# Pooled attention into a gated feed-forward layer: one matmul for each odd score, exponentials in groups of 16, even and odd tokens in turn

## The chip, the cores and the metric

One core of a Trainium2 chip runs the whole program. In this kernel TensorE does the matmuls, into buffers in PSUM memory; ScalarE does the exponentials and relu; VectorE and GpSimd do sums and products of elements. The metric is the device time of one execution in microseconds; the span of a profile, from the first to the last instruction of the core, is about 1.8 us shorter. Runs come in states; only fast runs are compared here, and of read_fours, a single run of unknown state, only the trace is read.

## The reference, cut to what matters

```python
# q, k, v: (8 batches, 8 heads, 576 tokens, 64)
k_p = k.reshape(B, H, Sp, 8, D).mean(axis=3)        # 72 pooled positions
v_p = v.reshape(B, H, Sp, 8, D).mean(axis=3)
scores = np.matmul(q, k_p.transpose(0, 1, 3, 2)) / np.sqrt(D)
attn = softmax(scores)                               # over 72 positions
x = np.matmul(attn, v_p)                             # -> (4608 tokens, 512)
out = (np.maximum(x @ w_gate, 0) * (x @ w_val)) @ w_out   # 512 -> 1536 -> 512
```

A caution about correctness: on these inputs the output has a standard deviation of 1.26e-5, and the spread between tokens of one batch is only 6.1e-8, half a per cent of that (computed from the reference). The comparison with the reference passes even when tokens of a batch are exchanged. A pass says little about the order of rows, which has to be checked by following the indices.

## The kernel before

A q tile holds two tokens side by side in the 128 rows: rows 0 to 63 are an even token, rows 64 to 127 the odd one after it. The pooled keys are kept twice, with zeros in the upper or the lower half, so that one matmul scores the even tokens (`j == 0`) and another the odd ones (`j == 1`). A batch has 18 column groups of 16 columns; 16 of these make the full blocks, 2 are the leftover. The value matmuls take blocks of 128 tokens as weights, and each block must lie in one piece. The leftover block takes 32 even and 32 odd tokens, and so the odd half stores its leftover first, next to the even one. That is why an odd score was two matmuls: its columns come in another order than they lie in q.

```python
def scores(b, h, j):
    n = RI * QP                                       # 2 * 16 = 32
    ...
    parts = ((n, 0, NF * IQ), (0, NF * IQ, RI)) if j else ((0, 0, NI),)
    ps = ps_at.tile([P, 512], F32, name="at_ps", tag="at_ps")
    for c0, i0, cnt in parts:                         # odd: 256 columns, then 32
        nc.tensor.matmul(
            out=ps[:SP, c0:c0 + cnt * QP], lhsT=kpTs[b % 2][j][:, h, :],
            rhs=queries(b, h, i0, cnt), start=True, stop=True)
    e = exp_tiles[b, h][:SP, j * HS:(j + 1) * HS]
    ...                                               # batch 7: two permuted views
    for out_ap, in_ap in views:
        nc.scalar.activation(out=out_ap, in_=in_ap, func=AF.Exp, scale=EXP_SCALE)

def weights(b, h, t):                                 # the weights of value block t
    ...
    n_blk, j = divmod(t, 2)                           # a block is all even or all odd
    c0 = NF * P if t == n_pc - 1 else (HS + RI * QP if j else 0) + n_blk * P
    return exp_tiles[b, h][:SP, c0:c0 + n]
```

Batch 0 goes another way and is not touched. Scores of a batch are put in groups of two (batch 1) or mostly three (later batches) between the matmuls of the feed-forward part.

The softmax here doesn't subtract the row's maximum and nothing guards it: scores larger than these inputs give would overflow.

## Time and profile before

| | before |
|---|---|
| median of the first 3 runs | 328.61 us (328.54 to 330.12) |
| TensorE busy | 318.7 us, 97% |
| ScalarE busy | 151.2 us, 46% |
| scores, batches 1 to 7, between starts of matmuls | 15.39 us |
| exponentials, batches 1 to 6 | 96 of 288 elements, 402 ns each |

The prediction below shows the lines of the page, the groups and the timeline. One view more: what TensorE waited for in the kernel before (who waited for whom: us in total, times, longest).

```profile
PE acc_ps L523 <- DVE sum L514: 0.3, 1, 0.3
PE at_ps L311 <- ACT expT L325: 0.2, 1, 0.2
```

The first line is a place where VectorE is the later one; the second is all that TensorE ever waited for an exponential.

### The profile page before, as it was taken

How to read it: one execution, taken by the hardware profiler on the slowest of the kernel's cores; microseconds unless marked ns; L12 is line 12 of the kernel's file. 1: busy time of each engine (PE TensorE's matmuls, PEld its weight loads, DVE VectorE, ACT ScalarE, POOL GpSimd, SP SyncE). 2: the span in 40 equal slices, each digit the busy share in tenths (PEclk: the TensorE clock that was granted, in tenths of full speed). 3: DMA queues.
4: the chain of work that ended last, by engine and by line, in shares of the span. 5: the costliest groups of instructions: out<-in, count | busy, mean ns of one | idle time of the engine just before them, and what ended most of it. 6: DMA issues, size and time to landing. Idle time of an engine off the chain costs nothing.

```text
span 327.4 us, 7013 instructions
## 1 busy us (share of the span) xinstructions
PE 318.7 (97%) x2670; PEld 226.9 (69%) x2670; DVE 226.2 (69%) x482; ACT 151.2 (46%) x353; POOL 206.9 (63%) x258
## 2 busy tenths in 40 slices
PE   8899999999999999999999999999999999999995
PEld 3577885455566656665898867655667888888674
DVE  7465737677684864696387745784779989879762
ACT  1454482364466226612672257225825565565330
POOL 8556607999999942965199309999901577667300
PEclk9999999999999999999999999999999999999999
DMA  7999998996958538999794472223012130130035
GB/s 110 186 203 202 200 211 151 200 173 118 187 101 159 100 91 86 78 154 160 159 169 76 87 104 60 33 47 124 3 24 50 34 96 2 22 111 2 10 112 137
DMA packets 51010, 35.46 MB, mean 108 GB/s; under 512 B 30432, under 2 KB 45024, under 8 KB 50976
## 3 DMA queue, kind: packets, MB, share of 16 engines
q0 software_dynamic: 18304, 18.88, 36.5%
q1 hardware_dynamic: 32528, 16.00, 26.2%
q8 instruction: 21, 0.34, 0.4%
q10 hardware_dynamic: 144, 0.13, 0.1%
q14 instruction: 13, 0.11, 0.1%
HBM read 37.75 MB, written 9.44 MB: 144 GB/s over the span
## 4 chain that ended last, share of the span: by engine, by line
PE 89%; DVE 6%; DMA 2%; issue 1%; POOL 1%; ACT 0%; DVEq 0%; POOLq 0%
PE mm_ps L430 42%; PE acc_ps L523 19%; PE mm_ps L742 9%; PE at_ps L311 4%; PE mm_ps L468 3%; PE at_ps L389 3%; PE mm_ps L602 2%; DMA q<-in_q_dram 2%; PE at_ps L742 2%; DVE px L395 1%; DVE sum L514 1%; DVE h L439 1%; PE mm_ps L412 1%; PE mm_ps L366 1%; DVE px L758 1%
## 5 line engine op out<-in xcount | busy, mean ns | idle before, releaser
L439 DVE TENSOR_TENSOR h<-mm_ps,relu 128x512 f16<-128x512 f32 (+1 forms) x96 | 59.8, 624 | 69.5 <-PE mm_ps L430 59.2
L436 ACT ACTIVATE relu<-mm_ps 128x512 f16<-128x512 f32 (+1 forms) x96 | 52.2, 544 | 100.1 <-PE mm_ps L430 94.6
L430 PE MATMUL mm_ps<-x_T,wv_sb 128*128 128x512 f16 (+1 forms) x432 | 88.4, 332 | 0.4 <-DVE kpT0u L264 0.4
L430 PE MATMUL mm_ps<-x_T,wg_sb 128*128 128x512 f16 (+1 forms) x432 | 88.5, 331 | 0.0
L430 PEld LDWEIGHTS <-wv_sb 128*128 128x128 f16 x432 | 42.1, 98 | 31.2 <-DVE kpT0u L264 0.8
L430 PEld LDWEIGHTS <-wg_sb 128*128 128x128 f16 x432 | 38.9, 97 | 19.7 <-issue 0.3
L325 ACT ACTIVATE expT<-at_ps 72x288 f16<-72x288 f32 (+2 forms) x128 | 38.8, 374 | 14.3 <-PE at_ps L311 14.2
L523 PEld LDWEIGHTS <-sum 128*128 128x128 f16 x336 | 32.0, 98 | 6.3 <-DVE sum L514 0.9
L395 DVE TENSOR_TENSOR px<-at_ps,prd 128x256 f16<-128x256 f32 (+1 forms) x80 | 33.8, 423 | 2.7
L181 POOL TENSOR_TENSOR tree_b<-tree_a 72x256 f32<-72x256 f32 (+1 forms) x42 | 33.5, 797 | 3.3
L764 POOL TENSOR_TENSOR h<-px 128x256 f16<-128x256 f16 x36 | 25.4, 718 | 13.8 <-ACT px L761 12.8
L175 POOL TENSOR_TENSOR tree_a<-k_in 96x512 f32<-96x512 f16 x18 | 21.5, 1196 | 15.2 <-DMA k_in<-in_k_dram 15.2
L523 PE MATMUL acc_ps<-wo_sums,sum 128*128 128x256 f16 x252 | 30.9, 272 | 0.0
L175 POOL TENSOR_TENSOR tree_a<-v_in 72x512 f32<-72x512 f16 x24 | 28.7, 1197 | 0.1
L523 PEld LDWEIGHTS <-h 128*128 128x128 f16 x252 | 23.7, 98 | 2.9
L763 POOL TENSOR_SCALAR px<-px 128x256 f16<-128x256 f16 x12 | 13.0, 1080 | 18.1 <-PE mm_ps L742 15.3
L844 POOL COPY gate<-h 128x1 f16<-128x1 f16 x4 | 1.5, 380 | 33.9 <-DVE h L439 33.9
L523 PE MATMUL acc_ps<-wo_sb,h 128*128 128x256 f16 x168 | 20.6, 272 | 0.0
L514 DVE TENSOR_TENSOR sum<-h 128x768 f16<-128x768 f16 x28 | 19.0, 679 | 0.0
L531 DVE TENSOR_TENSOR rows<-acc_ps,mid 128x512 f32<-128x512 f32 x21 | 14.4, 686 | 4.7 <-PE acc_ps L523 4.6
L389 PEld LDWEIGHTS <-expT 72*128 72x128 f16 (+1 forms) x280 | 12.9, 100 | 5.9 <-DVE prd L394 0.8
L394 DVE RECIPROCAL prd<-at_ps 128x4 f32<-128x4 f32 (+1 forms) x80 | 13.7, 171 | 3.7 <-PE at_ps L389 3.6
(144 smaller groups left out, 527.9 us busy)
## 6 DMA issues: line engine op xcount, KB each, us to landing
out_dram<-rows SPq DMA_DIRECT2D x24, 256.0 KB
k_in<-in_k_dram POOLq DMA_DIRECT2D x7, 576.0 KB, 7.0
q<-in_q_dram POOLq DMA_DIRECT2D x7, 576.0 KB, 10.0
v_in<-in_v_dram POOLq DMA_DIRECT2D x6, 576.0 KB, 12.7
wg_sb<-in_moe_w_gate_dram POOLq DMA_DIRECT2D x6, 256.0 KB, 11.0
wv_sb<-in_moe_w_val_dram POOLq DMA_DIRECT2D x6, 256.0 KB, 10.8
wo_sb<-in_moe_w_out_dram POOLq DMA_DIRECT2D x3, 512.0 KB, 10.7
v_in<-in_v_dram POOLq DMA_DIRECT2D x2, 512.0 KB, 11.9
```

What stands on the lines that cost most here:

```text
L175: eng.tensor_tensor(out=cell["a"][:n], in0=src[:, :, :4 * D], in1=src[:, :, 4 * D:], op=ALU.add)
L181: eng.tensor_tensor(out=cell["c"][:n], in0=a[:n, :, :2 * D], in1=a[:n, :, 2 * D:], op=ALU.add)
L325: nc.scalar.activation(out=out_ap, in_=in_ap, func=AF.Exp, scale=EXP_SCALE)
L389: nc.tensor.matmul(out=ps[:n, c0:c0 + D + 1], lhsT=weights(b, h, t), rhs=stats[b % 2][:SP, g, s0:s0 + D + 1], start=True, stop=True,)
L395: nc.vector.tensor_tensor(out=x[:n, half * NG // 2:(half + 1) * NG // 2, :, :], in0=pv.rearrange("p g (x c) -> p g x c", x=2)[:, :, :, :D] ...
L430: nc.tensor.matmul(out=t[:, lo:hi], lhsT=w[:, ci, fsl], rhs=x_T[:, ci, x0:x0 + hi - lo], start=(ci == 0), stop=(ci == n_co - 1),)
L436: nc.scalar.activation(out=relu[:, :n], in_=ps[0][:, :n], func=AF.Relu)
L439: nc.vector.tensor_tensor(out=h_tiles[c][:, fo, t0:t0 + n], in0=ps[1][:, :n], in1=relu[:, :n], op=ALU.mult)
L514: nc.vector.tensor_tensor(out=S[k][:, i], in0=x[:, i], in1=y[:, i], op=op)
L523: nc.tensor.matmul(out=ps[:, tb, :], lhsT=lhs[:, i, tb * P:(tb + 1) * P], rhs=rhs[:, i, :], start=(first and tb == 0 and i == 0), stop=(tb ...
L742: nc.tensor.matmul(out=ps[key][:, m], lhsT=w_of(m)[:, i], rhs=xs[:, i], start=(first and m == 0 and i == 0), stop=(m == 1 and i == N_CO - ...
L764: nc.gpsimd.tensor_tensor(out=hc[:, fo_out, cols], in0=gv[:, 0], in1=gv[:, 1], op=ALU.mult)
```

## The change

Its intent is that an odd score is one matmul, as an even one is. The exponentials of a head are stored as 18 groups of 16 even, 16 odd tokens, so any block of 128 columns holds both kinds and the leftover is simply the end. The price: each activation writes 16 elements, leaves out 16, and so on (in batch 7: every second element), and the rows of the output go to other places.

```diff
-        parts = ((n, 0, NF * IQ), (0, NF * IQ, RI)) if j else ((0, 0, NI),)
-        ps = ps_at.tile([P, 512], F32, name="at_ps", tag="at_ps")
-        for c0, i0, cnt in parts:
-            nc.tensor.matmul(... queries(b, h, i0, cnt) ...)
-        e = exp_tiles[b, h][:SP, j * HS:(j + 1) * HS]
+        ps = ps_at.tile([P, 512], F32, name="at_ps", tag="at_ps")[:SP, :HS]
+        nc.tensor.matmul(
+            out=ps, lhsT=kpTs[b % 2][j][:, h, :], rhs=queries(b, h), start=True, stop=True)
+        e = exp_tiles[b, h][:SP]
+        def blocks(cols):
+            return e[:, cols].rearrange("s (i j p) -> s i j p", j=2, p=QP)[:, :, j]
+        ps = ps.rearrange("s (i p) -> s i p", p=QP)
+        views = [(blocks(slice(0, 2 * HS)), ps)]
         if b == LAST:
+            views = [(blocks(rest), ps[:, i:]),
+                     (e[:, full].rearrange("s (t p i j) -> s t p i j", ...)[:, :, :, :, j],
+                      ps[:, :i].rearrange("s (t i) p -> s t p i", i=TP // 2))]
 ...
-        c0 = NF * P if t == n_pc - 1 else (HS + RI * QP if j else 0) + n_blk * P
-        return exp_tiles[b, h][:SP, c0:c0 + n]
+        return exp_tiles[b, h][:SP, t * P:t * P + n]
 ... (stores: rows of a block are now neighbours in memory; the leftovers of a
      batch are one store of 64 rows where they were two of 32)
```

More of the change, by code (lines that the diff above doesn't have):

```diff
@@ L108 @@
     out_rows_of = out.rearrange("(b p i j) d -> b j i p d", j=2, i=NI, p=QP)
-    out_cols_of = out.rearrange("(b p i j) d -> b j p i d", j=2, i=NI, p=QP)
+    out_runs_of = out.rearrange("(b p r) d -> b r p d", r=QT, p=QP)
+    out_cols_of = out.rearrange("(b p r) d -> b p r d", r=QT, p=QP)
+    TP = P // QP
     def full_at(b):
@@ L301, in scores @@
     def scores(b, h, j):
-        n = RI * QP
         if j == 0:
@@ L307, in scores @@
                 "s j p -> s (j p)")
-        parts = ((n, 0, NF * IQ), (0, NF * IQ, RI)) if j else ((0, 0, NI),)
-        ps = ps_at.tile([P, 512], F32, name="at_ps", tag="at_ps")
-        for c0, i0, cnt in parts:
-            nc.tensor.matmul(
-                out=ps[:SP, c0:c0 + cnt * QP], lhsT=kpTs[b % 2][j][:, h, :],
-                rhs=queries(b, h, i0, cnt), start=True, stop=True,
-            )
-        e = exp_tiles[b, h][:SP, j * HS:(j + 1) * HS]
-        ps = ps[:SP, :HS]
-        views = [(e, ps)]
-        if b == LAST:
-            rest = slice(0, n) if j else slice(HS - n, HS)
-            full = slice(n, HS) if j else slice(0, HS - n)
-            views = [(e[:, rest], ps[:, rest]),
-                     (e[:, full].rearrange("s (k p i) -> s k p i", k=NF, i=IQ),
-                      ps[:, full].rearrange("s (k i p) -> s k p i", k=NF, i=IQ))]
+        ps = ps_at.tile([P, 512], F32, name="at_ps", tag="at_ps")[:SP, :HS]
+        nc.tensor.matmul(
+            out=ps, lhsT=kpTs[b % 2][j][:, h, :], rhs=queries(b, h), start=True, stop=True)
+        e = exp_tiles[b, h][:SP]
+        full, rest = slice(0, 2 * NF * P), slice(2 * NF * P, None)
+        def blocks(cols):
+            return e[:, cols].rearrange("s (i j p) -> s i j p", j=2, p=QP)[:, :, j]
+        ps = ps.rearrange("s (i p) -> s i p", p=QP)
+        views = [(blocks(slice(0, 2 * HS)), ps)]
+        if b == LAST:
+            i = 2 * NF * P // (2 * QP)
+            views = [(blocks(rest), ps[:, i:]),
+                     (e[:, full].rearrange("s (t p i j) -> s t p i j", p=QP, j=2, i=TP // 2)[
+                         :, :, :, :, j],
+                      ps[:, :i].rearrange("s (t i) p -> s t p i", i=TP // 2))]
         for out_ap, in_ap in views:
@@ L331, in weights @@
             return pieces[t][:SP, h, :n]
-        n_blk, j = divmod(t, 2)
-        c0 = NF * P if t == n_pc - 1 else (HS + RI * QP if j else 0) + n_blk * P
-        return exp_tiles[b, h][:SP, c0:c0 + n]
+        return exp_tiles[b, h][:SP, t * P:t * P + n]
     def pool_v_array(b, half):
@@ L445, in store @@
         if rest % P == (REST if b % 2 else 0) and (b % 2 or rest < FULL):
-            n, j = divmod((r0 - full_at(b)) // P, 2)
-            nc.sync.dma_start(out=out_rows_of[b, j, n * IQ:(n + 1) * IQ], in_=o)
+            t = (r0 - full_at(b)) // P
+            n, j = divmod(t, 2)
+            to = out_runs_of[b, t * TP:(t + 1) * TP] if b else \
+                out_rows_of[b, j, n * IQ:(n + 1) * IQ]
+            nc.sync.dma_start(out=to, in_=o)
         else:
             half = RI * QP
-            for x in range(4):
-                nc.sync.dma_start(
-                    out=out_rows_of[b + x // 2, x % 2, NF * IQ:], in_=o[x * half:(x + 1) * half])
+            for x in range(2):
+                if b + x:
+                    nc.sync.dma_start(
+                        out=out_runs_of[b + x, 2 * NF * TP:], in_=o[x * REST:(x + 1) * REST])
+                    continue
+                for j in range(2):
+                    nc.sync.dma_start(
+                        out=out_rows_of[0, j, NF * IQ:], in_=o[j * half:(j + 1) * half])
     def store_cols(o, t, eng, cols):
-        n, j = divmod(t, 2)
-        eng.dma_start(out=out_cols_of[LAST, j, :, n * IQ:(n + 1) * IQ, cols], in_=o)
+        eng.dma_start(out=out_cols_of[LAST, :, t * TP:(t + 1) * TP, cols], in_=o)
     def out_rows(c, ts, eng=None):
```

## The prediction

> **What bounds the kernel now.** I read first the busy shares and the chain that ended last on the page, because they say which engine's time is the kernel's time.
>
> ```profile
> PE 318.7 (97%) x2670; PEld 226.9 (69%) x2670; DVE 226.2 (69%) x482; ACT 151.2 (46%) x353; POOL 206.9 (63%) x258
> ...
> PE 89%; DVE 6%; DMA 2%; issue 1%; POOL 1%; ACT 0%; DVEq 0%; POOLq 0%
> ```
>
> TensorE is busy for 97% of the span and carries 89% of the chain; ScalarE is busy for 46% and carries none of it. A busy TensorE is not proof of a bound, since ends of matmuls are modelled, so the second view is busy time by stretch, over the stretches in which batches 2 to 7 are scored (columns: stretch, length, then busy time and count of PE, PEld, DVE, ACT, POOL, granted clock, DMA share, GB/s).
>
> ```profile
> 80.00:120.00 40.00, 39.95 (x311) 24.38 (x308) 29.72 (x66) 17.21 (x37) 35.92 (x46) 1.00 0.70 129
> 120.00:160.00 40.00, 40.00 (x303) 25.76 (x302) 25.19 (x49) 18.12 (x38) 19.63 (x25) 1.00 1.03 131
> 200.00:240.00 40.00, 39.73 (x297) 24.71 (x296) 26.41 (x50) 19.60 (x60) 35.73 (x33) 1.00 0.18 42
> ```
>
> TensorE has no gap there, at full clock, and the list of waits gives TensorE only 0.2 us of waiting on ScalarE in the whole run. So what the change saves on TensorE should come off the end nearly in full, and what it costs ScalarE should be hidden. The third view says how big the thing removed is: the groups of the scores, each shape apart.
>
> ```profile
> L311 PE MATMUL at_ps<-qT,kpT1l 128*72 128x288 f16 x32 | 9.1, 290 | 0.0
> L311 PE MATMUL at_ps<-qT,kpT1u 128*72 128x256 f16 x32 | 8.7, 273 | 0.2 <-ACT expT L325 0.2
> ...
> L311 PE MATMUL at_ps<-qT,kpT1u 128*72 128x32 f16 x32 | 5.7, 179 | 0.0
> ...
> L311 PE MATMUL at_ps<-qT,kpT0u 128*72 128x32 f16 x24 | 4.3, 179 | 0.0
> ```
>
> The trap is here. The two groups of 32 columns, 32 + 24 = 56 matmuls, show 5.7 + 4.3 = 10.0 us of busy time. That is not what they cost: 179 ns is the latency of one, and the next matmul starts long before it ends. What a matmul costs a full TensorE is the distance to the next start, which the timeline shows (start, length, engine, line, operation; "x2" is the pair of 256 and 32 columns of one odd score).
>
> ```profile
> 127.39 0.29 PE L311 MATMUL at_ps<-qT,kpT0l 128*72 128x288 f16 x1
> 127.51 0.29 PE L311 MATMUL at_ps<-qT,kpT0u 128*72 128x256 f16 x2
> 127.65 0.29 PE L311 MATMUL at_ps<-qT,kpT0l 128*72 128x288 f16 x1
> 127.78 1.03 PE L430 MATMUL mm_ps<-x_T,wg_sb 128*128 128x512 f16 x4
> 128.64 1.03 PE L430 MATMUL mm_ps<-x_T,wv_sb 128*128 128x512 f16 x4
> 129.51 0.29 PE L311 MATMUL at_ps<-qT,kpT0u 128*72 128x256 f16 x2
> ```
>
> An even score (one matmul of 288 columns) holds TensorE for 127.51 - 127.39 = 0.12 us, an odd one (two matmuls) for 127.65 - 127.51 = 0.14 us. The even score after it takes 0.13. The removed matmul is worth some hundredths of a microsecond each, not 0.18.
>
> **What the Trainium skill says.** "TensorE: Matmul & The Clock Gate", section "Wait — 56ns, not 53.3ns?", has warm matmuls start N/2.4 GHz + about 2.5 ns apart, and never closer than about 25 ns however small N is. This trace agrees: the starts, read to the nanosecond, are 123 ns apart after 288 columns (288/2.4 + 2.5 = 122.5), 109 after 256 (109.2), and 28 after 32 columns, where the formula alone would give 15.8: the floor. "ScalarE: Activation LUTs", section "What ACT_TABLE_LOAD costs", has an activation with immediate operands take 186 ns + 0.833 ns per element, with about 93 ns overlapped back to back. For 288 that is 426, and 333 in a row; the trace has 402 and, between starts in a row, 290, a little less. "SBUF — State Buffer", section "Door 1: The DMA port swizzle", says that SBUF works in lines of 16 bytes and that at least two hits per line keep full bandwidth. No instruction of this trace writes groups as short as the new ones, so the trace neither confirms nor denies it.
>
> **The change, part by part.**
>
> 1. Removed on TensorE: in each of 7 batches x 8 heads = 56 odd scores, the second matmul and its weight load. The built instruction order of the two kernels agrees: 112 rows fewer on TensorE. Before, an odd score costs 109 + 28 = 137 ns; after, as one matmul of 288 columns, 123. That is 14 ns x 56 = 0.78 us.
>
> 2. A shadow of it: the score that follows a 32-column matmul takes 129 ns rather than 123[...]. Thirty even scores follow an odd one directly: 6 ns x 30 = 0.18 us. Parts 1 and 2 make 0.96 us of a TensorE that has no gaps.
>
> 3. Moved on ScalarE: for batches 1 to 6 each exponential writes 18 groups of 16 f16 (32 bytes, with 32 bytes between them) rather than 288 in a row; for batch 7 it writes every second f16. Same count, same elements. The groups of the exponentials now:
>
> ```profile
> L325 ACT ACTIVATE expT<-at_ps 72x288 f16<-72x288 f32 x96 | 32.5, 402 | 13.0 <-PE at_ps L311 13.0
> ...
> L325 ACT ACTIVATE expT<-at_ps 72x256 f16<-72x256 f32 x16 | 5.8, 384 | 0.0
> ```
>
> The 256-element form of batch 7 already reads PSUM with a stride of 64 bytes, and its successor starts 264 ns later, which is 290 - 32 x 0.833 = 263: a strided read costs nothing. For the write, 16 f16 fill two whole 16-byte lines, and every second f16 still leaves four per line, so by the page above both stay at full rate. I choose no change, and at most 10%. The tightest place for ScalarE is batch 1, where two scores follow every half-size gate and value pair:
>
> ```profile
> 43.47 0.70 ACT L325 ACTIVATE expT<-at_ps 72x288 f16<-72x288 f32 x2 [0.16 <-PE at_ps L311]
> 44.07 0.38 ACT L436 ACTIVATE relu<-mm_ps 128x256 f16<-128x256 f32 x1
> 44.60 0.70 ACT L325 ACTIVATE expT<-at_ps 72x288 f16<-72x288 f32 x2 [0.16 <-PE at_ps L311]
> ```
>
> The period is 44.60 - 43.47 = 1.13 us, with 0.16 us idle. Two exponentials take 2 x 0.29 = 0.58 us of it, so they would have to slow by 0.16/0.58 = 28% before ScalarE set the pace even there. Elsewhere three of them and one 0.6 us relu share 2.1 us or more.
>
> 4. Moved in waits: a block of values now holds even and odd tokens, so the first block of batches 2, 4 and 6 needs the last odd exponential too; in the built order just three weight loads gain a wait on ScalarE. In these batches a whole gate and value unit (1.7 us) lies between the last score and the first value block, against an exponential of 0.4 us and a relu of 0.6. It costs 0.
>
> 5. Output: 7 fewer stores of the small kind (four of 32 rows become two of 64), the same 2 KB rows, now adjacent in memory. The queue that issues them mostly waits for data, and only the last store is on the path: same size, 1 KB pieces as before. It costs 0.
>
> Sum: 0.96 us off. I let a tenth of it be absorbed in the few places where TensorE waits on VectorE anyway (0.35 us at 65 us is one), so 0.9: 328.61 - 0.9 = 327.7 us, 0.3%.
>
> **Rivals.** (a) The busy-time reading: 56 x 179 ns = 10 us off, 318.6. Against it stands the 0.14 against 0.12 us of the timeline; I give it nearly nothing. (b) The scattered write is slow. If each element cost twice as much, an exponential would grow by 0.24 us; in batch 1 a pair and its relu would need about 0.58 + 0.48 + 0.38 = 1.4 us against 1.13, 0.3 us x 8 rounds = 2.4 us later, and batch 7, with 0.36 us idle of each 2.13 us period, would lose about 1 more: 331, 1% slower. Only the missing precedent for such a write speaks for it. (c) Nothing comes through: each saving of 40 ns per trio is swallowed by the next wait, 328.6. The gapless stretches speak against it. (d) Stores to adjacent rows land sooner or later than before: they are hidden, at most 0.3 us at the tail either way.
>
> **Range and chances.** The three runs of before span 328.54 to 330.12, so noise of some tenths is as large as the effect. 327.0 to 328.8 holds the sum in full, nothing, and a small loss. Neither side reaches 2% (6.6 us) by any step worked out here: faster 0.01, same 0.97, slower 0.02.
>
> **What would show it.** Right: the 32-column groups are gone, all 112 scores have one shape, a trio falls from 0.39-0.40 to 0.37 us between starts, the exponentials still take about 0.40 us, and TensorE's waits on ScalarE stay near 0.2 us. Wrong: exponentials of 0.45 us and more, starts in a row over 0.32 us, a wait of TensorE on ScalarE of more than 1 us in batch 1 or 7, or a saving of TensorE over 2 us.

## The result, and the profile after

| | before | after |
|---|---|---|
| median, fast runs of these rounds | 328.88 us (4 runs) | 327.90 us (4 runs) |
| ratio, 95% interval | | 0.9968 (0.9948 to 0.9988) |
| the same in a second set of rounds | 329.10 us (11 runs) | 328.29 us (5 runs), 0.9972 (0.9958 to 0.9986) |

A ratio here is formed from the fast runs of the same rounds; it is not quite the ratio of the medians. The changed kernel is 0.3% faster: clear of noise, and "same" by a limit of 2%.

The page of the changed kernel, busy shares and chain:

```profile
PE 316.8 (97%) x2614; PEld 224.7 (69%) x2614; DVE 226.6 (69%) x482; ACT 151.9 (47%) x353; POOL 206.2 (63%) x258
...
PE 88%; DVE 6%; DMA 2%; issue 1%; ACT 1%; POOL 1%; DVEq 0%; ACTq 0%; POOLq 0%
```

There are 2670 - 2614 = 56 matmuls fewer, and the bound is where it was. TensorE's busy time fell by 1.9 us, the span of this execution by 0.9: as the prediction warned, busy time of matmuls is no measure of what they cost. Of the 1.9 us, 1.1 lie in the 28 warm-up matmuls at the start (10.1 us before, 9.0 after), which the change does not touch. The groups of the odd scores in the changed kernel, by form:

```profile
L310 PE MATMUL at_ps<-qT,kpT1u 128*72 128x288 f16 x32 | 8.9, 287 | 0.2 <-ACT expT L327 0.2
...
L310 PE MATMUL at_ps<-qT,kpT0u 128*72 128x288 f16 x24 | 6.6, 286 | 0.0
```

The rows of 256 and of 32 columns are gone. The timeline of the first group of batch 4 answers to that of the prediction (start, length, what):

```profile
127.17 0.29 PE L310 MATMUL at_ps<-qT,kpT0l 128*72 128x288 f16 x1
127.29 0.29 PE L310 MATMUL at_ps<-qT,kpT0u 128*72 128x288 f16 x1
127.42 0.29 PE L310 MATMUL at_ps<-qT,kpT0l 128*72 128x288 f16 x1
127.54 1.03 PE L430 MATMUL mm_ps<-x_T,wg_sb 128*128 128x512 f16 x4
```

Three scores hold TensorE for 127.54 - 127.17 = 0.37 us, where it was 127.78 - 127.39 = 0.39. Taking each score's distance to the next matmul from the starts in the trace, all 112 scores took 15.39 us before and 14.40 after: 0.99 us less, in which the waits inside the stages are counted too. The stretches from a batch's first score to the first matmul after its last one sum to 68.62 us before and 67.67 after, 0.95 us less.

On ScalarE, the exponentials of batches 1 to 6 and of batch 7:

```profile
L327 ACT ACTIVATE expT<-at_ps 72x288 f16<-72x288 f32 x96 | 32.6, 403 | 12.6 <-PE at_ps L310 12.0
L327 ACT ACTIVATE expT<-at_ps 72x256 f16<-72x256 f32 x16 | 6.5, 461 | 0.0
```

Groups of 16 cost nothing: 403 ns against 402, and 290 ns between starts in a row as before. Batch 7's did slow down, from 384 to 461 ns, and from 264 to 304 ns between starts. Nobody waits for it: TensorE's waits of the changed kernel have the same line for exponentials as before.

```profile
PE acc_ps L530 <- DVE sum L521: 0.7, 2, 0.3
...
PE at_ps L310 <- ACT expT L327: 0.2, 1, 0.2
```

The first line is the small part of the gain that did not arrive. TensorE now waits 0.7 us for VectorE's sums rather than 0.3, because it comes there earlier while VectorE's work is what it was. Of the six stretches from the end of one batch's scores to the start of the next, the two with these waits grew from 22.51 to 22.66 us and from 22.58 to 22.63: 0.20 us given back. after_again shows 22.66 and 22.62. The sum of all six is no such witness: it was 129.99 us before, 130.14 after, and 129.78 in after_again, because the first stretch alone was 18.55, 18.49 and 18.15 us.

### The profile page after: what moved, and what is told of

Same layout as the page of the kernel before. It is cut to its first block, busy times and chain, and to the rows that moved or that the text cites. A ratio compares the mean times of both kernels' runs of the same rounds, so it can differ in the third digit from the quotient of the medians.

```text
span 326.5 us, 6890 instructions
## 1 busy us (share of the span) xinstructions
PE 316.8 (97%) x2614; PEld 224.7 (69%) x2614; DVE 226.6 (69%) x482; ACT 151.9 (47%) x353; POOL 206.2 (63%) x258
## 4 chain that ended last, share of the span: by engine, by line
PE 88%; DVE 6%; DMA 2%; issue 1%; ACT 1%; POOL 1%; DVEq 0%; ACTq 0%; POOLq 0%
PE mm_ps L430 42%; PE acc_ps L530 19%; PE mm_ps L749 9%; PE at_ps L310 4%; PE mm_ps L475 3%; PE at_ps L389 3%; PE mm_ps L609 2%; PE at_ps L749 2%; DMA q<-in_q_dram 2%; DVE px L395 1%; DVE sum L521 1%; DVE h L439 1%; PE mm_ps L412 1%; DVE px L765 1%; PE mm_ps L284 1%
## 5 line engine op out<-in xcount | busy, mean ns | idle before, releaser
L430 PEld LDWEIGHTS <-wg_sb 128*128 128x128 f16 x432 | 40.0, 98 | 20.7 <-issue 0.4
L327 ACT ACTIVATE expT<-at_ps 72x288 f16<-72x288 f32 (+2 forms) x128 | 39.7, 384 | 13.4 <-PE at_ps L310 12.7
## 6 DMA issues: line engine op xcount, KB each, us to landing
wo_sb<-in_moe_w_out_dram POOLq DMA_DIRECT2D x3, 512.0 KB, 10.1
```

What stands on the lines that cost most here:

```text
L430: nc.tensor.matmul(out=t[:, lo:hi], lhsT=w[:, ci, fsl], rhs=x_T[:, ci, x0:x0 + hi - lo], start=(ci == 0), stop=(ci == n_co - 1),)
```

## The experiments

Theory: the saving is the TensorE time of 56 small matmuls and nothing else, and the new way of writing is hidden behind TensorE. Rivals: the saving comes from the stores to adjacent rows or from the layout; ScalarE is near its limit and only just hides the new writes. All ratios are against the kernel before of the same rounds.

**after_again: the changed kernel once more**, without an edit.

> The changed kernel once more, to narrow the interval. If the saving is the 0.96 us of TensorE counted in the prediction and nothing else, the ratio to the kernel before is 0.997 (0.9 to 1.0 us less). If the first measurement was noise, the ratio lies within 0.001 of 1.

Ratio 0.9972 (0.9958 to 0.9986), five runs of 327.88 to 328.47 us against eleven of 328.51 to 329.92. The saving is not noise.

**split_odd: undo only the merging.**

```diff
+        cut = NF * IQ
+        for i0, cnt in ((0, cut), (cut, RI)) if j else ((0, NI),):
+            nc.tensor.matmul(
+                out=ps[:, i0 * QP:(i0 + cnt) * QP], lhsT=kpTs[b % 2][j][:, h, :],
+                rhs=queries(b, h, i0, cnt), start=True, stop=True)
```

> The changed kernel with one thing undone: each odd score is two matmuls again (256 and 32 columns), the layout of the exponentials, the blocks and the stores stay new. Theory (the matmul count is the whole saving): the scores take 15.4 us between starts again instead of 14.4, and the time goes back to that of the kernel before, ratio 0.999 to 1.001. Rival (the saving comes from the stores to adjacent rows, or from the new layout): the ratio stays at 0.997.

Ratio 0.9998 (0.998 to 1.0015); the scores take 15.40 us between starts, the score stages 68.62 us, both as in the kernel before. The first group of batch 4 holds TensorE for 128.25 - 127.86 = 0.39 us again:

```profile
127.86 0.29 PE L312 MATMUL at_ps<-qT,kpT0l 128*72 128x288 f16 x1
127.99 0.29 PE L312 MATMUL at_ps<-qT,kpT0u 128*72 128x256 f16 x2
128.12 0.29 PE L312 MATMUL at_ps<-qT,kpT0l 128*72 128x288 f16 x1
128.25 1.03 PE L433 MATMUL mm_ps<-x_T,wg_sb 128*128 128x512 f16 x4
```

With new layout and new stores but two matmuls, the saving is gone. The rivals of stores and layout fall.

**merge_only: do only the merging**, in the kernel before.

```diff
-        parts = ((n, 0, NF * IQ), (0, NF * IQ, RI)) if j else ((0, 0, NI),)
+        parts = ((0, 0, NI),)
```

> The kernel before with one thing done: an odd score is one matmul of 288 columns, layout and stores stay old. The odd tokens land in wrong blocks, so the result is wrong on purpose. Theory: the whole saving, ratio 0.997, scores 14.4 us between starts. Rival (stores or layout): ratio 1.000.

Ratio 0.9983 (0.9966 to 1.0; one of six runs was slow and is left out). By its time alone this run decides nothing, since the interval holds both 0.997 and 1. The trace is plainer: the scores take 14.40 us between starts and the stages 67.67 us, the same as in the changed kernel. In the profiled execution half a microsecond was lost elsewhere; the view of waits has a line that neither of the two kernels has.

```profile
PE mm_ps L430 <- DMA x_T<-px: 0.4, 1, 0.4
```

This is a transposing transfer that landed late once. Whether it did so in the other runs the times don't say.

**split_all: a double dose**, every score of the changed kernel in two matmuls.

```diff
+        for i0, cnt in ((0, cut), (cut, RI)):
```

> The changed kernel with every score split into 256 and 32 columns, even ones too: a double dose of what the change removed. Theory: 112 small matmuls at 14 ns net each and a shadow of about 6 ns on the matmul after each is 2.2 us more than the changed kernel, 1.2 us more than the kernel before: ratio 1.003 to 1.004. Rival (the split costs nothing, the layout does): ratio 0.997. Busy-time rival (179 ns for each): ratio above 1.03.

Ratio 1.0003 (0.9989 to 1.0017): the expected size was missed. The timeline shows that the dose itself was taken, three scores now from 127.81 to 128.23, 0.42 us:

```profile
127.81 0.29 PE L312 MATMUL at_ps<-qT,kpT0l 128*72 128x256 f16 x2
127.94 0.29 PE L312 MATMUL at_ps<-qT,kpT0u 128*72 128x256 f16 x2
128.09 0.29 PE L312 MATMUL at_ps<-qT,kpT0l 128*72 128x256 f16 x2
128.23 1.02 PE L433 MATMUL mm_ps<-x_T,wg_sb 128*128 128x512 f16 x4
```

The score stages sum to 69.58 us, 1.91 more than in the changed kernel (2.2 was expected, with 6 ns of delay behind each of the 112 small matmuls; the trace has such a delay mainly where another score follows directly, 66 times, where 256 columns take 115 or 116 ns rather than 109). Of that the time shows some 1.0 us. The waits for VectorE's sums, 0.7 us in the changed kernel, are not in this kernel's list of waits at all, and the stretches in which they lie shrank from 22.66 and 22.63 us to 22.25 and 22.14, by 0.41 and 0.49. So VectorE is a second limit close behind TensorE in two of the six stretches between the scores: what one makes TensorE slower, up to about 0.4 us a stretch, comes back there, and what one makes it faster is in part lost there.

**step_two and read_fours: which side of batch 7's activation became slow.** It reads PSUM in fours with a stride of 64 bytes (before: in eights), and it writes every second f16 (before: in a row). step_two gives the write alone to batches 1 to 6; read_fours leaves batch 7 the read alone. Both leave tokens in wrong places.

```diff
 # step_two
-        views = [(blocks(slice(0, 2 * HS)), ps)]
+        views = [(e.rearrange("s (i p j) -> s i p j", j=2, p=QP)[:, :, :, j], ps)]
 # read_fours
-                     (e[:, full].rearrange("s (t p i j) -> s t p i j", ...)[:, :, :, :, j],
+                     (e[:, j * NF * P:(j + 1) * NF * P].rearrange(
+                         "s (t p i) -> s t p i", p=QP, i=TP // 2),
```

> The changed kernel, but in batches 1 to 6 each exponential reads PSUM in a row and writes every second f16, as batch 7 does; the stores are left, so the order of the rows is wrong on purpose. It asks which side of batch 7's activation made its successor start 303 ns later instead of 264. If the write at every second f16 is it (39 ns for 256 elements), the 288-element ones go from 290 to about 334 ns between starts and from 403 to about 490 ns each. If the read in fours from PSUM is it, they stay at 290 and 403. In both cases ScalarE has slack and the ratio stays at 0.997.

> The changed kernel, but in batch 7 the exponential of 256 elements writes them in a row while it still reads PSUM in fours with a stride of 64 bytes; wrong values on purpose. If the write at every second f16 costs the 39 ns, the time between starts goes back to 264 and its length to about 383; if the read in fours costs it, they stay at 303 and 460.

The groups of the exponentials, step_two first (its batches 1 to 6), then read_fours (its batch 7):

```profile
L327 ACT ACTIVATE expT<-at_ps 72x288 f16<-72x288 f32 x96 | 38.0, 483 | 11.1 <-PE at_ps L310 10.2
```

```profile
L327 ACT ACTIVATE expT<-at_ps 72x256 f16<-72x256 f32 x16 | 5.8, 385 | 0.0
```

With the write at every second f16, 288 elements take 483 ns rather than 403, and 322 to 334 between starts in a row, most often 326, rather than 290 or 291. Without it, batch 7 is back at 385 and 264. It is the write. The time of step_two is 0.9976 (0.9959 to 0.9992), as good as the changed kernel's: even 96 slowed exponentials are hidden. Its score stage of batch 1, the tightest for ScalarE, is 8.46 us against 8.38, so some 36 ns more per exponential are just felt there.

**exp_twice_b1: a dose for ScalarE where it is tightest.**

```diff
-        for out_ap, in_ap in views:
+        for out_ap, in_ap in views * (2 if b == 1 else 1):
```

> The changed kernel, with each exponential of batch 1 done twice to the same place: a dose of 2 x 290 ns in each of 8 periods of 1.13 us in which ScalarE is idle for 0.16. The prediction's claim is that ScalarE sets the pace once a pair grows by more than 0.16 us. Then each period grows by 0.58 - 0.16 = 0.42 us, 2.5 to 3.4 us in all: ratio 1.005 to 1.008. If ScalarE is not near its limit there, the ratio stays at 0.997.

Ratio 1.0316 (1.0278 to 1.0355): the sign was right, the size far off. The local part came as expected: the score stage of batch 1 grew from 8.38 to 11.65 us, by 3.27. The rest of it is in the waits of TensorE.

```profile
PE at_ps L310 <- DMA qT<-q: 6.0, 1, 6.0
PE at_ps L310 <- ACT expT L327: 2.7, 6, 0.7
```

The second line is the delay that was put in. The first is new: batch 2's queries, transposed by a transfer, are not there. The chain of waits shows the transfer and what follows it (start, length, what):

```profile
58.72 17.33 DMA qT<-q
76.05 0.04 issue
76.09 0.88 PE at_ps L310 x3
76.97 2.56 PE mm_ps L475 x6
```

In the changed kernel this transfer is issued at 54.6 us and nobody waits for it at 66.0. Here it is issued at 58.7 and lands only 17.3 us later, in a stretch in which the DMA engines are full (shares of 0.93 and 1.22 in the view by stretch). But they are hardly less full in the changed kernel (0.88 to 1.01 from 54.6 to 76 us). What differs is the order: there the transfer is issued 3.1 us before the next loads of k, q and v from GpSimd's queue (57.7, 58.2 and 58.8 us), here in their midst (58.3, 58.8 and 59.4). In its first 4.1 us there, the transfer's queue (q1) has 70% of the DMA engines' time and GpSimd's (q0) 6%; in its first 7.3 us here, 25% and 68%. And while TensorE waits, its granted clock falls: it is 0.50 from 76 to 80 us, where six matmuls of 512 columns take 2.56 us instead of 1.30. A delay of 3.3 us became 11 us. No run isolates what made the transfer slower; that the loads were no longer behind it is the likely cause, and this is argued from the two traces, not shown.

**half_array: an attempt to beat both**, without the zeros: even scores on the lower 64 rows of the array, odd ones on the upper 64.

```diff
+        ds = slice(D, P) if j else slice(0, D)
         nc.tensor.matmul(
-            out=ps, lhsT=kpTs[b % 2][j][:, h, :], rhs=queries(b, h), start=True, stop=True)
+            out=ps, lhsT=kpTs[b % 2][j][ds, h, :], rhs=queries(b, h)[ds], start=True, stop=True)
```

> The changed kernel, but an even score uses only the lower 64 rows of the array and an odd one only the upper 64 (the other half of the weights was zeros), so neighbours may run side by side: an attempt to beat it. In the trace of before the one kind of matmul on 64 rows (pooling the values of batch 1) starts 93 ns late and delays the next by 120. There are 8 + 36 groups of scores. If neighbours run side by side, 39 of them are saved at 123 ns (4.8 us) against 44 x 213 ns = 9.4 us for changing the shape: 4.6 us slower than the changed kernel, ratio about 1.011. If they do not, 9 us slower, ratio 1.025. If the changes of shape cost nothing, ratio 0.983.

Ratio 1.0116 (1.0096 to 1.0136), as in the first of the three cases. The timeline shows both sides of the bargain.

```profile
128.54 1.03 PE L431 MATMUL mm_ps<-x_T,wv_sb 128*128 128x512 f16 x4
129.49 0.31 PE L311 MATMUL at_ps<-qT,kpT0l 64*72 64x288 f16 x1
129.50 0.31 PE L311 MATMUL at_ps<-qT,kpT0u 64*72 64x288 f16 x1
129.64 0.28 PE L311 MATMUL at_ps<-qT,kpT0l 64*72 64x288 f16 x1
129.86 1.04 PE L431 MATMUL mm_ps<-x_T,wg_sb 128*128 128x512 f16 x4
```

The first two scores start 4 ns apart (129.494 and 129.498 us) and so run side by side. But the group starts late (the last of the four matmuls before it holds the array for 309 ns instead of 216), the second lasts 146 ns until the third starts, the third takes 215 ns instead of 123, and the group as a whole is no shorter than three plain scores: 129.86 - 129.49 = 0.37 us. The pairs are too few for each change of the array's shape. "TensorEngine Tiling (Array Packing)" in the Trainium skill, section "Key Properties", says that changing the tiling mode drains TensorE, without a number; here the delay is 93 ns going in and some 90 to 120 coming out.

**rest_wide and rest_wide_v: the same cost, found elsewhere and taken away.** The leftover block of each batch loads 64 columns of weights, the only value block that does. In the changed kernel, the last matmul before it holds TensorE for 309 ns (512 columns alone take 216) and its own last one for 130 instead of 32. In rest_wide, the leftover is the first 64 tokens of a batch, and its weight load takes the next 64 columns along; their results are never read. rest_wide_v also gives 128 rows to the 64-row matmul that pools values.

```diff
-        full, rest = slice(0, 2 * NF * P), slice(2 * NF * P, None)
+        full, rest = slice(REST, None), slice(0, REST)
-        return exp_tiles[b, h][:SP, t * P:t * P + n]
+        c0 = 0 if t == n_pc - 1 else REST + t * P
+        return exp_tiles[b, h][:SP, c0:c0 + P]
-                    out=ps[:n, c0:c0 + D + 1], lhsT=weights(b, h, t),
+                    out=ps[:P if b else n, c0:c0 + D + 1], lhsT=weights(b, h, t),
 ... (stores and the views of batch 7 shifted by the leftover's 4 rows)
 # rest_wide_v, besides:
+        nc.vector.memset(rest[P // 2:], 0.0)
-            out=ps[:SP], lhsT=sel_rest[:P // 2], rhs=rest[:, hs, :], start=False, stop=True)
+            out=ps[:SP], lhsT=sel_rest, rhs=rest[:, hs, :], start=False, stop=True)
```

> An attempt to beat the changed kernel with what the traces show beside the change. The block of the 64 leftover tokens is the one value block that loads 64 columns of weights rather than 128; in all traces TensorE starts it 96 ns late and the matmul after it 98 ns late, in each of batches 1 to 7. Here the leftover tokens are the first of a batch, and the weight load takes them together with the next 64 columns, whose results nobody reads, so the shape of the array is never changed. If the change of shape is the cause: 7 x 194 ns = 1.36 us less than the changed kernel, ratio about 0.993. If the small block itself is the cause: ratio 0.997.

> The same, and the matmul on 64 rows that pools the last values of batches 0 and 1 is given 128 rows (the upper 64 zero). The two of batch 1 cost 93 + 120 ns each in the traces: 0.43 us less than the kernel with wide leftovers, ratio about 0.9917; those of batch 0 lie in the start, which waits for data.

rest_wide: median 326.48 us, ratio 0.9928 (0.9912 to 0.9944). rest_wide_v: median 326.04 us, ratio 0.9906 (0.9891 to 0.9921). The timeline of batch 2's leftover block, in the changed kernel and then in rest_wide_v:

```profile
91.55 1.03 PE L430 MATMUL mm_ps<-x_T,wv_sb 128*128 128x512 f16 x4
92.50 0.45 PE L389 MATMUL at_ps<-stat,expT 72*64 72x65 f16 x8
92.88 1.04 PE L430 MATMUL mm_ps<-x_T,wg_sb 128*128 128x512 f16 x4
```

```profile
90.28 1.03 PE L433 MATMUL mm_ps<-x_T,wv_sb 128*128 128x512 f16 x4
91.15 0.41 PE L392 MATMUL at_ps<-stat,expT 72*128 72x65 f16 x8
91.39 1.03 PE L433 MATMUL mm_ps<-x_T,wg_sb 128*128 128x512 f16 x4
```

From the gate and value matmuls to the next ones is 92.88 - 91.55 = 1.33 us with 64 columns of weights and 91.39 - 90.28 = 1.11 with 128, for the same eight matmuls. The change of shape is the cause, and both kernels are beaten: rest_wide_v saves three times what the change did. Two things are said with less certainty. Of the 1.8 us between the profiles of the changed kernel and rest_wide (326.5 and 324.7), 1.35 are the seven changes of shape; part of the rest is luck with VectorE, since a wait of 0.48 us near 219 us is gone and one near 95 us has grown by 0.23. And how a change of shape costs is open: the trace shows the load of the 64 columns starting only with its matmul (92.502 and 92.504 us), where otherwise a load starts with the matmul before (127.171, for a matmul at 127.292). So the delay may be a drain, or only a weight load (96 to 114 ns here) that is not taken ahead; no run tells these apart. The order of the rows of the changed kernel and of the wide leftovers was checked by following the indices, for the reason given with the reference.

## Why the prediction was right, point by point

- **The bound and the trap of busy time.** Right in the main. The 10.0 us of busy time in the small matmuls were worth 0.99 us. Three readings were loose. The stretches shown leave out batches 2 and 5 (scored from 66 to 76 and from 161 to 171 us). The list of waits has two lines of 0.2 us on ScalarE, one of them for exponentials. And "no gap" hid waits for VectorE's sums: measured between starts, the matmuls that read them came 0.37 us late near 118 us and 0.43 near 220 in the kernel before, of which only 0.32 shows as idle time; the busy time of the matmul before covers the rest.
- **Part 1 and 2, 0.78 + 0.18 = 0.96 us off TensorE.** Right: 0.99 us between starts, 0.95 us in the score stages, and exactly undone and redone by split_odd and merge_only. All but 5 of the 112 scores now take 121 to 123 ns. The shadow was there (28 scores of 129 or 130 ns before), but no run shows why. Behind a 32-column matmul only matmuls with 72 columns of weights took longer, that is scores and two that pool values (116 ns for 256 columns); those with 128 columns of weights did not (215 ns for 512 columns, 108 or 109 for 256).
- **Part 3, ScalarE.** Right for batches 1 to 6 (402 to 403 ns). Wrong for batch 7: "no change, and at most 10%" was 20% longer each and 15% more between starts. The step that failed is the one that took four values in a 16-byte line for enough; step_two and read_fours put the whole of it on the write. Nor is it so that no instruction of the trace writes groups this short: eight casts of VectorE (kpT, L233) write groups of 8, though none of ScalarE does. It is off the path: 16 x 40 ns, 0.6 us in all, behind a busy TensorE.
- **The slack of ScalarE in batch 1.** The arithmetic (0.16 us of 1.13) gave 2.5 to 3.4 us for the dose of exp_twice_b1, and the stage took 3.27. What it left out is what a late stage does to a transfer and to the clock.
- **Part 4 and 5, waits and stores at no cost.** Right: TensorE waits as little for exponentials as before, and split_odd, with all new stores, is as fast as the kernel before.
- **A tenth absorbed.** The right kind, and too small: 0.20 of 0.95 us went into TensorE's waits for VectorE's sums. That part was chosen, not derived, and that the time came so near is partly luck; split_all shows where it goes.
- **The time.** 327.7 was predicted, 327.9 measured in the first rounds and 328.3 in the second. The kernel before drifted by the same amounts (328.6, 328.9, 329.1), so the ratio, 0.3% as predicted, is the better witness.

## What to carry to other kernels

Price a matmul by the distance to the next start, not by its busy time: here the second was ten times the first. Before making small matmuls fewer, look for those that change the array's shape, with 64 rows or columns of weights among neighbours with 128: each cost about 200 ns here, in and out, seven times the 28 ns of a small matmul of 32 columns. The scores' 72 columns of weights cost no such delay. And where TensorE is the bound by a hair, a saving is given back at the next engine in line; a double dose in the other direction shows how near it is.

## What the Trainium skill lacked or had wrong

- "SBUF — State Buffer", section "Door 1: The DMA port swizzle": two hits in a 16-byte line should keep full bandwidth, so 16-bit elements could be strided freely up to 8. A ScalarE write of every second f16, four in a line, took 326 ns between starts for 288 elements instead of 290 (304 instead of 264 for 256). Groups of 16 in every 32 were free, as the page has it.
- "TensorEngine Tiling (Array Packing)", section "Key Properties": it says that a change of tiling mode drains TensorE but gives no cost. Here it was 93 to 97 ns before the matmuls with 64 rows or 64 columns and 90 to 121 ns after them; no run shows that a drain is what takes this time. Two matmuls on the two halves of the array's rows started 3 or 4 ns apart; "TensorE: Matmul & The Clock Gate", section "Measured speedup vs the span model", has about 4 ns for each further tile.
- "TensorE: Matmul & The Clock Gate", section "Wait — 56ns, not 53.3ns?": the floor of about 25 ns was 28 here, each matmul with its own weight load; no page has that a score right after such a short one took 6 to 7 ns longer (129 instead of 123, 116 instead of 109).
- "ScalarE: Activation LUTs", section "What ACT_TABLE_LOAD costs": 186 ns + 0.833 ns per element gives 426 for 288, and 333 in a row; 402 and 290 were measured.
- No page gives a figure for how a transposing transfer slows beside other loads: the same transfer, issued 4 us later and amid three loads, landed after 17.3 us, and TensorE waited 6.0 us for it.
